# A planned attention and two-layer kernel: another bank for row transposes, regrouped sums, weight words moved, and the attention's norm shared and opened to ScalarE

## The chip, the core and the metric

One Trainium2 chip, one core. The metric is device microseconds of the whole program, median of the runs; the profiled execution is one more run, recorded by the hardware profiler, and it has a time of its own. Engines by their names in the profile: PE (TensorE's matmuls), PEld (its weight loads), DVE (VectorE), ACT (ScalarE), POOL (GpSimd), SP (SyncE, which issues nearly all DMAs here).

## What is computed

The reference, cut to what matters (`q`, `k`, `v` are 4 x 8 x 768 x 64; `x` is 3072 x 512; `w_in` 512 x 2048, `w_out` 2048 x 512, all float64 but the attention's inputs):

```python
for c in range(24):                      # chunks of 32 queries, with 8 memory keys
    k_full = concat(mem_k, k[max(0, 32*c - 16) : 32*c + 40])
    scores = (q_c @ k_full.T) / 8
    a = exp(scores - max(scores)); a = a / (sum(a) + 1e-9)
    out_c = a @ v_full
x = attention, as 3072 tokens x 512
h = x @ moe_w_in;  g = h * tanh(softplus(h));      x = g @ moe_w_out     # layer 1
h = x @ moe2_w_in; g = h * sigmoid(1.702 * h);     x = g @ moe2_w_out    # layer 2
```

The weights arrive as float64. The kernel takes their 32-bit words apart, rebuilds a float32 from them, and splits each float32 operand into a high and a low fp32r part; a product is then three matmuls (high x high, low x high, high x low).

## The kernel before

The program has four stages in time, on PE almost back to back.

- **Stage A** (to about 415 us): attention and layer 1's first product. `forward(j, f)` is one unit: 12 matmuls of 128x384 for token block j (8 blocks of 384) and column block f (16). It cycles over four PSUM banks, `h` twice, `o2`, `o3`. The attention of block j+1 runs between the units of block j, by *octs* (two heads x four windows of 96 queries) for j >= 2 and by *quads* (half an oct) for j < 2. An oct's steps are `oct_scores` (8 matmuls, L717), `quad` twice (mask and minimum on DVE, L758; four exponentials on ACT with their sums, L773; `plus` and `inverse`, L791 and L795, which turn the sums into factors; `norm`, L798, one DVE multiplication of 96x512, or `norm_act`, L807, four ACT instructions of 96x128), and `oct_out` (transposes L904, copies L911 or L913, values L924, and the split into `xh` and `xl`). For j >= 2 the norm could go to DVE alone.
- **Stage B** (about 415 to 685 us): layer 1's second product, `second(1, k)`, 12 units of 256 tokens. A unit is one 2x2 Winograd product: four blocks `a11`, `a12`, `a21`, `a22` are loaded from `g1d` and put through Mish on ACT, sums of them are formed by `comb` (L1226), each operand is split (L1235 or L1236, and L1238), and seven steps of 24 matmuls of 128x256 (L1248) run on PE. Step 1 writes bank `o3` (`hd`). At a unit's end `row` transposes its two result rows (tiles `ev` for the lower, `u` for the upper; four transposes each, L1268) into `o3` and `o2`; a copy to `u` (L1129 on ACT or L1130 on DVE) empties the bank and a DMA stores the row to `x1d`.
- **Stage C** (about 685 to 915 us): layer 2's first product, `first(q)`, 32 units of seven products (L1159).
- **Stage D** (to the end): layer 2's second product, `second(2, k)`, 12 units of the same seven steps, without Mish and without transposes.

`w_words(layer, part, p, ...)` makes one *set of words*: two loads of 512 KB of float64 weights, two conversions (a scaling on ACT, L346, or on DVE, L349; three integer operations on DVE, L355, L359, L363), four sums on DVE (L415), and in most sets four stores to `wd`. Twelve sets are placed in stage A (one every seven forward units from the 20th), six in stage B, six in stage C.

Order is set by `Plan`. Each operation has a rank, one or two ways (engine, cost), and tiles that it reads and writes; a tag such as `vt=2` says how many tiles rotate. `Plan.issue` plays the program through with those costs, picks on each engine the ready operation of the lowest rank, takes the second way only where the first engine's queue is long enough, and then emits everything in the order found. Each engine then works strictly in that order.

```python
bank = T[("o2", "o3")[th]].new([P, KD, P], F32)      # row(): th = 0 upper, 1 lower row
hd = T["o3"].new([P, H2], F32)                       # second(): step 1's bank
a11 = block(0, "vt", r - 2.6);  a22 = block(3, own[0], r - 1.9)
a21 = block(2, "vt", r - 1.2);  a12 = block(1, own[3], r - 0.6)
ways = [("dve", dve(4 * P), norm), ("act", 4 * act(P), norm_act)]
add(rank + 1.4, ways if j < EARLY else ways[:1], reads=[r, done], updates=[e])
```

Of the kernel before, what the change touches and what calls it, by code (L numbers as in the profile page):

```python
# [9 lines left out]
F32 = mybir.dt.float32  # L10
F32R = mybir.dt.float32r
I32 = mybir.dt.int32
AF = mybir.ActivationFunctionType
# [228 lines left out]
def kernel(  # L242
# [478 lines left out]
        add(rank + 0.5, [("pe", 1.4, scores)], reads=pair[0][2], writes=s)  # L721
        return s

    def quad(j, hp, gp, heads, rank, given=None):
        b, s0 = divmod(j * TB, S)
        g0 = s0 // GQ + 2 * gp
        queries, keys, turned_from = heads
# [6 lines left out]
        mx, sm = T["mx"].new([GQ, 2, 2], F32), T["sm"].new([GQ, 2, 2], F32)  # L734
        r = T["r"].new([GQ, 2, 2, 1], F32)
        done = fixed()

        def scores():
# [33 lines left out]
        def power(i, hh):  # L772
            nc.scalar.activation(  # L773
                out=e[:, i, hh, :],
                in_=e[:, i, hh, :],
                func=AF.Exp,
                scale=-1.0,
                bias=mx[:, i, hh:hh + 1],
                accum_out=sm[:, i, hh:hh + 1],
            )  # L780

        for i in range(2):
# [3 lines left out]
                    reads=[e, mx], writes=[done, sm], table="exp",  # L786
                )

        def plus():
            r3 = r.get().rearrange("p a b o -> p a (b o)")  # L790
            nc.vector.tensor_scalar(out=r3, in0=sm.get(), scalar1=1e-9, scalar2=None, op0=ALU.add)  # L791

        def inverse():
            r3 = r.get().rearrange("p a b o -> p a (b o)")
            nc.vector.reciprocal(out=r3, in_=r3)  # L795

        def norm():
            nc.vector.tensor_tensor(  # L798
                out=e.get(), in0=e.get(), in1=r.get().to_broadcast([GQ, 2, 2, P]), op=ALU.mult
            )  # L800

        add(rank + 1.4, [("dve", 0.23, plus)], reads=[sm], writes=[r])
        add(rank + 1.4, [("dve", 0.16, inverse)], updates=[r])
        def norm_act():
            for i in range(2):
                for hh in range(2):
                    nc.scalar.activation(  # L807
                        out=e[:, i, hh, :], in_=e[:, i, hh, :], func=AF.Copy, scale=r[:, i, hh, :]
                    )
# [136 lines left out]
    def quads():  # L946

        last = None
        for j in range(NB):
# [4 lines left out]
            for n in range(NQ):  # L954
                rank = base + 2 * n
                if j < EARLY:
                    gp, hp = divmod(n, H // 2)
                    if hp == 0:
                        st = rows_of_heads(j, gp, rank)
                    heads, vals = turned(j, hp, st, rank), st[2]  # L960
                else:
                    hp, gp = divmod(n, GB // 2)
                    if gp == 0:
                        pair = pair_of_heads(j, hp, rank)
                        if 2 * hp % HV == 0:
# [3 lines left out]
                        oct_out(j, hp, vals, rank, names, [  # L969
                            quad(j, hp, i, pair[i], rank + STAGGER * i, s)[1] for i in range(GB // 2)  # L970
                        ])
# [233 lines left out]
    def second(layer, k):  # L1205
# [93 lines left out]
        comb(r + 1.6, a22, a22, a11, ALU.subtract)  # L1299
        step(4, 1, a22, hb, False)  # L1300
        copy(r + 4.1, View(u2), hb, H2)
        step(5, 3, a11, hb, False)
        plus(r + 5.05, bottom, p5, hb)
        plus(r + 5.06, bottom, p4, hb, 0)
        row(1, bottom)
        comb(r + 2.4, a12, a12, a22, ALU.subtract)
        step(6, 6, a12, hc, False)
        plus(r + 6.1, top, u2, hc)
        row(0, top)
# [23 lines left out]
    for j in range(NB):  # L1333
        for f in range(NF):
# [4 lines left out]
            forward(j, f)  # L1339
            i = j * NF + f  # L1340
            n, rest = divmod(i - NF - 4, 7)
            if rest == 0 and 0 <= n < 12:
                layer, p = ((1, 4), (1, 5), (1, 6), (1, 7), (1, 0), (1, 1), (1, 2), (2, 0), (2, 1), (2, 2), (2, 3), (1, 3))[n]
# [8 lines left out]
            if i >= L1 - NF + 6 and f % 2 == 0:  # L1352
                w_out(1, f // 2 - 2, i + 1)
    w_out(1, 6, L1 + 0.5)
    for k1 in range(3 * NS):
        second(1, k1)
        if k1 % 2 == 0:
            p = (4, 5, 6, 7, 14, 15)[k1 // 2]
            w_words(2, p // NP, p % NP, RB[1] + 7 * k1 + 6, [pace[1, k1]], ("v", "v"))
# [54 lines left out]
```

## Time and profile before

| | |
|---|---|
| runs shown | 1161.67, 1163.86, 1165.37 us; median 1163.86 |
| profiled execution | 1165.48 us, its span 1163.7 us |
| PE busy | 1124.6 us (97%) |
| DVE busy | 867.2 us (75%) |
| ACT busy | 612.2 us (53%) |
| mean granted clock | 0.987 |
| chain that ended last | PE 87%, DMA 4%, DVE 3% |

PE's busy time and the chain both say that the program is PE's work from end to end; what is left to gain lies in PE's idle stretches and in the stretches in which its clock is at the lower of its two levels (1.2 instead of 2.4 GHz). The granted clock is given as a share of 2.4 GHz. A matmul's duration in the trace contains its way through the array, so two matmuls in a row overlap; what one costs is the distance from start to start.

### The profile page before, as it was taken

The numbers are of one execution on the slowest core, as the hardware profiler recorded it, in microseconds if no ns is written. First come the engines' busy times: TensorE is split into PE (matmuls) and PEld (weight loads), VectorE is DVE, ScalarE is ACT, GpSimd is POOL, SyncE is SP. The second block draws the span as 40 slices with busy tenths as digits, with TensorE's granted clock in tenths as the row PEclk, the third lists the DMA queues.
The fourth block names the chain that finished last, engine by engine and source line by source line (L and its number), as shares of the span: only waits on it lengthen the run. The fifth ranks groups of instructions, "written<-read, shape, count | busy, mean of one in ns | idle before, by whom it ended". The sixth has DMA issues, their size and how long they took to land.

```text
span 1163.7 us, 22807 instructions
## 1 busy us (share of the span) xinstructions
PE 1124.6 (97%) x8352; PEld 1091.0 (94%) x8352; DVE 867.2 (75%) x1975; ACT 612.2 (53%) x1416; POOL 15.1 (1%) x34
## 2 busy tenths in 40 slices
PE   7888999999999999999999899999999999999998
PEld 6677999999998999999999899999999999999998
DVE  5898878887876478788788876756466868787875
ACT  5775554565545446566565566556555534333332
POOL 2000000000000000000000000000000000000000
PEclk9899999999999999999999899999999999999999
DMA  9945778767894674754655577777878663635452
GB/s 210 263 128 141 198 213 245 206 158 206 239 245 123 184 210 127 207 165 128 204 168 154 177 232 243 236 255 228 261 243 267 208 172 101 163 109 157 116 138 62
DMA packets 325743, 217.97 MB, mean 187 GB/s; under 512 B 136120, under 2 KB 300743, under 8 KB 325631
## 3 DMA queue, kind: packets, MB, share of 16 engines
q1 hardware_dynamic: 325279, 215.76, 64.8%
q8 instruction: 66, 1.08, 0.4%
q0 software_dynamic: 352, 0.75, 0.3%
q14 instruction: 46, 0.38, 0.1%
HBM read 135.18 MB, written 81.26 MB: 186 GB/s over the span
## 4 chain that ended last, share of the span: by engine, by line
PE 87%; DMA 4%; DVE 3%; SPq 2%; ACT 2%; issue 1%; DVEq 0%; ACTq 0%
PE o L1248 18%; PE o L1004 12%; PE h L1004 11%; PE s L1248 11%; PE h L1248 11%; PE h L1159 8%; PE o L1159 7%; PE s L1159 3%; SPq L305 2%; PE o L717 1%; PE s L717 1%; PE o L924 1%; PE s L924 1%; PE s L904 1%; DMA vt<-in_v_dram 1%
## 5 line engine op out<-in xcount | busy, mean ns | idle before, releaser
L1004 PE MATMUL h<-xh,wi 128*128 128x384 f32 x384 | 102.3, 347 | 0.9 <-DVE gh L1130 0.8
L1004 PE MATMUL o<-xh,wi 128*128 128x384 f32 x384 | 101.6, 346 | 0.0
L773 ACT ACTIVATE e<-e,mx 96x128 f32<-96x128 f32 x240 | 93.1, 390 | 15.3 <-DVE mx L758 15.2
L1248 PE MATMUL o<-wo,xh 128*128 128x256 f32 x456 | 87.9, 288 | 6.8 <-ACT u L1129 4.2
L1238 DVE TENSOR_TENSOR xl<-wi,xh 128x1024 fp32r<-128x1024 f32 x64 | 77.8, 1220 | 6.7 <-ACT xh L1235 6.0
L1248 PEld LDWEIGHTS o<-wo,xh 128*128 128x128 f32 x456 | 72.3, 195 | 8.7 <-ACT u L1129 5.6
L1238 DVE TENSOR_TENSOR xl<-vt,xh 128x1024 fp32r<-128x1024 f32 x48 | 58.6, 1221 | 21.3 <-ACT xh L1235 20.6
L1004 PEld LDWEIGHTS h<-xh,wi 128*128 128x128 f32 x384 | 68.9, 191 | 3.6 <-ACT st L346 0.9
L1004 PEld LDWEIGHTS o<-xh,wi 128*128 128x128 f32 x384 | 69.7, 192 | 1.2
L1235 ACT ACTIVATE xh<-wi 128x1024 fp32r<-128x1024 f32 x51 | 53.9, 1058 | 29.2 <-PE h L1248 10.7
L1248 PE MATMUL o<-wo,xl 128*128 128x256 f32 x228 | 66.0, 290 | 1.2 <-DVE xl L1238 1.2
L1004 PE MATMUL o<-xl,wi 128*128 128x384 f32 x192 | 65.1, 339 | 0.0
L1004 PE MATMUL h<-xl,wi 128*128 128x384 f32 x192 | 65.1, 339 | 0.0
L1248 PE MATMUL s<-wo,xh 128*128 128x256 f32 x312 | 59.9, 287 | 1.2 <-DVE xh L1236 1.2
L1248 PE MATMUL o<-wi,xh 128*128 128x256 f32 x312 | 58.8, 282 | 0.0
L1248 PE MATMUL o<-wo,wi 128*128 128x256 f32 x342 | 48.4, 283 | 4.1 <-ACT u L1129 2.0
L1248 PEld LDWEIGHTS s<-wo,xh 128*128 128x128 f32 x312 | 49.4, 194 | 1.6 <-DVE xh L1236 1.6
L1248 PEld LDWEIGHTS o<-wo,wi 128*128 128x128 f32 x342 | 43.4, 188 | 6.2 <-ACT u L1129 2.7
L1129 ACT ACTIVATE e<-h 128x384 f32<-128x384 f32 (+1 forms) x50 | 22.4, 448 | 49.3 <-PE h L1248 37.9
L1248 PEld LDWEIGHTS o<-wi,xh 128*128 128x128 f32 x312 | 48.2, 190 | 0.0
L1248 PE MATMUL h<-wi,xh 128*128 128x256 f32 x256 | 47.6, 282 | 0.0
L1248 PE MATMUL h<-wo,xh 128*128 128x256 f32 x256 | 47.3, 281 | 0.0
(410 smaller groups left out, 3163.9 us busy)
## 6 DMA issues: line engine op xcount, KB each, us to landing
st<-in_moe_w_out_dram SPq DMA_DIRECT2D x32, 512.0 KB
st<-wd SPq DMA_DIRECT2D x29, 512.0 KB
g1d<-gh SPq DMA_DIRECT2D x64, 192.0 KB
g1d<-gl SPq DMA_DIRECT2D x64, 192.0 KB
vt<-g1d SPq DMA_DIRECT2D x24, 512.0 KB
wi<-g1d SPq DMA_DIRECT2D x24, 512.0 KB
vt<-gd SPq DMA_DIRECT2D x24, 512.0 KB
wi<-gd SPq DMA_DIRECT2D x24, 512.0 KB
```

Source lines behind the costliest of these rows:

```text
L305: queue.dma_start(out=o, in_=i)
L717: nc.tensor.matmul(out=s[hh][:, keys(d, i, True), :], lhsT=queries(d, i), rhs=keys(d, i), start=True, stop=True)
L773: nc.scalar.activation(out=e[:, i, hh, :], in_=e[:, i, hh, :], func=AF.Exp, scale=-1.0, bias=mx[:, i, hh:hh + 1], accum_out=sm[:, i, hh:hh ...
L904: nc.tensor.transpose(t[:, i, hh, :], e[:, i, hh, :], ident[:GQ, :GQ])
L924: nc.tensor.matmul(out=o[hh * D:(hh + 1) * D, g], lhsT=vt[:, g, h + hh], rhs=aTs[g // 2][:, g % 2, hh], start=True, stop=True,)
L1004: nc.tensor.matmul(out=h.get(), lhsT=a[:, c], rhs=b.at(kk), start=(n == 0), stop=(n == 3 * KD - 1))
L1129: ("act", act(n, True), lambda: nc.scalar.activation(out=dst(), in_=bank.get(), func=AF.Copy)),
L1159: nc.tensor.matmul(out=bank.get(), lhsT=a, rhs=b, start=(fresh and m == 0), stop=(m == 3 * K2 - 1), skip_group_check=not fresh,)
L1235: ("act", act(NP * P), lambda: nc.scalar.activation(out=flat(gh), in_=flat(src), func=AF.Copy)),
L1238: add(rank + 0.05, [("dve", dve(NP * P), lambda: nc.vector.tensor_tensor(out=flat(gl), in0=flat(src), in1=flat(gh), op=ALU.subtract))], re ...
L1248: nc.tensor.matmul(out=bank.get(), lhsT=a[:, p], rhs=b, start=(fresh and p == 0 and m == 0), stop=(p == NP - 1 and m == 2), skip_group_che ...
```

## The change

Four edits.

1. `row` of layer 1 transposes both rows into bank `o2`; `o3` is left to `hd` (and to the forward units of stage A).
2. Layer 1's sums are written into other tiles: `a22` becomes a21+a22, then that minus a11; `a21` becomes a11-a21; `a11` itself is only read. Layer 2's sums stay.
3. Stage A makes 14 sets of words instead of 12 (sets (2, 4) and (2, 5), of layer 2's first weights, at forward units 104 and 111); stage B makes four instead of six, behind units 1, 3, 5, 7 instead of 0, 2, 4, 6, 8, 10.
4. In an oct, `sm` and `r` are shared by its two quads: `inverses` runs once, on 96x8, behind the exponentials of both; the norms follow, each on DVE or on ACT, for every j.

```diff
+    def inverses(rank, sm, r):
...
+        add(rank + 1.4, [("dve", 0.23, plus)], reads=[sm], writes=[r])
+        add(rank + 1.4, [("dve", 0.16, inverse)], updates=[r])
...
-        ways = [("dve", dve(4 * P), norm), ("act", 4 * act(P), norm_act)]
-        add(rank + 1.4, ways if j < EARLY else ways[:1], reads=[r, done], updates=[e])
+        def scaled():
+            add(rank + 1.4, [("dve", dve(4 * P), norm), ("act", 4 * act(P), norm_act)], reads=[r, done], updates=[e])
+
+        if both:
+            return e, scaled
+        scaled()
...
+                        both = [T[x].new([GQ, GB, 2], F32) for x in ("sm", "r")]
+                        es = [quad(j, hp, i, pair[i], rank + STAGGER * i, s, both) for i in range(GB // 2)]
+                        inverses(rank + STAGGER, *both)
+                        for _, scaled in es:
+                            scaled()
...
-            bank = T[("o2", "o3")[th]].new([P, KD, P], F32)
+            bank = T["o2"].new([P, KD, P], F32)
...
-        comb(r + 0.2, a11, a11, a21, ALU.subtract)
-        comb(r + 0.3, a21, a21, a22, ALU.add)
-        step(3, 4, a21, hc, True)
+        if layer == 1:
+            comb(r + 0.3, a22, a21, a22, ALU.add)
+            comb(r + 0.4, a21, a11, a21, ALU.subtract)
+            s1, s2, s3 = a22, a11, a21
...
+        step(3, 4, s1, hc, True)
...
+        comb(r + (1.2, 1.6)[layer - 1], s2, a22, a11, ALU.subtract)
+        step(4, 1, s2, hb, False)
...
+        step(5, 3, s3, hb, False)
...
+        comb(r + 2.4, a12, a12, s2, ALU.subtract)
...
-            if rest == 0 and 0 <= n < 12:
+            if rest == 0 and 0 <= n < 14:
...
+    WB = {1: (0, 6), 3: (0, 7), 5: (1, 6), 7: (1, 7)}
...
-        if k1 % 2 == 0:
-            p = (4, 5, 6, 7, 14, 15)[k1 // 2]
+        if k1 in WB:
```

What moves, at three places. **PE between two units of stage B** (the fourth and the fifth): before, the last matmul of the fourth unit, its upper row's transposes (`u` into `o2`), step 0 of the next unit (`s0`), the lower row's transposes (`ev` into `o3`), and step 1 of the next unit (`o3`).

```order
L1248 MATMUL h_6380<-wi15_5613,xl_6491 128x256
L1268 MATMUL o2_6587<-ident_64,u_6483 128x128 x4
L1248 MATMUL s0_6596<-wo7_2846,wi1_6582 128x256 x2
...
L1248 MATMUL s0_6596<-wo3_4998,wi2_6585 128x256
L1268 MATMUL o3_6628<-ident_64,ev_6594 128x128 x4
L1248 MATMUL o3_6645<-wo6_2997,xh_6592 128x256 x2
```

Now, from the end of the next unit's step 0 on:

```order
L1259 MATMUL s0_6589<-wo3_5169,wi2_6587 128x256
L1279 MATMUL o2_6623<-ident_64,ev_6614 128x128 x4
L1259 MATMUL o3_6628<-wo6_3038,xh_6616 128x256 x2
...
L1259 MATMUL o3_6628<-wi7_5440,xl_6619 128x256
L1279 MATMUL o2_6667<-ident_64,u_6472 128x128 x4
L1259 MATMUL s0_6589<-wo4_2943,xh_6660 128x256 x2
```

Before, step 1 came directly behind transposes into its own bank; now a whole step stands between the two groups of transposes, which share `o2`, and step 1's bank is touched by no transposes. All eleven places between units read so now; before there were two kinds, this one and one in which `ev` and `u` follow each other directly, with step 1 behind them.

**DVE in an oct of stage A** (`r` and `sm` are the factors and sums, `e` the exponentials; `u`, `st` belong to a set of words). Before, two quads, each with its own small operations and its norm:

```order
L791 TENSOR_SCALAR r<-sm 96x4
L359 SCALAR_TENSOR_TENSOR u<-st,u 128x512
L795 RECIPROCAL r<-r 96x4
L363 SCALAR_TENSOR_TENSOR u<-st,u 128x512
L798 TENSOR_TENSOR e<-e,r 96x512
L791 TENSOR_SCALAR r<-sm 96x4
L795 RECIPROCAL r<-r 96x4
L798 TENSOR_TENSOR e<-e,r 96x512
```

Now, an oct on DVE, and then ACT's rows around the other half of its norm (`gl` and `gh` are forward units' results):

```order
L727 TENSOR_SCALAR r<-sm 96x8
L359 SCALAR_TENSOR_TENSOR v<-st,v 128x512
L730 RECIPROCAL r<-r 96x8
L363 SCALAR_TENSOR_TENSOR v<-st,v 128x512
L804 TENSOR_TENSOR e<-e,r 96x512
```

```order
L784 ACTIVATE e,sm<-e,mx 96x128 x4
L1140 ACTIVATE gl<-h 128x384
L812 ACTIVATE e<-e,r 96x128 x4
L1140 ACTIVATE gh<-o_3659 128x384
```

One pair of small operations is left of two, and one of the two norms stands on ACT, behind the second quad's exponentials. Over the program 20 of the 48 quads of octs have their norm on ACT now (none before); the other 28 stay on DVE.

**PE at the end of the attention** (the last oct's scores L717, transposes L904, values L924; L1004 are forward units). Before:

```order
L717 MATMUL o_5169<-kT,qT 96x128
L1004 MATMUL o_5179<-xh,wi_1302 128x384 x2
...
L1004 MATMUL o_5206<-xl,wi_1374 128x384
L1248 MATMUL s_5240<-wo_2846,xh 128x256 x2
...
L1248 MATMUL s_5240<-wo_4998,xl 128x256
L904 MATMUL o_5270<-ident,e 128x96 x4
L904 MATMUL o_5275<-ident,e 128x96 x4
L924 MATMUL o_5284<-aT,vt 64x96 x8
L1004 MATMUL h<-xh,wi_576 128x384 x2
```

Now:

```order
L717 MATMUL o_5015<-kT,qT 96x128
L932 MATMUL s_5032<-aT,vt 64x96 x8
L1015 MATMUL h<-xh,wi_999 128x384 x2
...
L1015 MATMUL h<-xl,wi_1194 128x384
L912 MATMUL o_5162<-ident,e 128x96 x4
L912 MATMUL o_5171<-ident,e 128x96 x4
L1015 MATMUL h<-xh,wi_1233 128x384 x2
...
L932 MATMUL o_5199<-aT,vt 64x96 x8
L1015 MATMUL o_5215<-xh,wi_1302 128x384 x2
```

Before, two forward units and the first step of stage B (`s`, L1248) stood between the last scores and their transposes; now it is five forward units, a sixth lies between transposes and values, two more behind the values, and the step of stage B has gone behind the last forward unit.

## Rows read from the trace of the kernel before

**Rows 1.** Busy time by stretch: PE, PEld, DVE, ACT, POOL, clock, DMA share, GB/s.

```profile
100.00:200.00 100.00, 99.63 (x780) 93.97 (x780) 78.57 (x320) 52.16 (x200) 2.10 (x7) 0.99 0.76 207
450.00:650.00 200.00, 192.71 (x1604) 190.03 (x1603) 160.93 (x200) 119.77 (x154) 0.00 (x0) 1.00 0.57 166
940.00:1140.00 200.00, 199.89 (x1682) 199.63 (x1682) 154.80 (x160) 72.19 (x103) 0.00 (x0) 1.00 0.48 133
```

**Rows 2.** Waits of PE, 430 to 690 us (total, times, longest); PE in order of time.

```profile
PE o L1248 <- ACT u L1129: 6.2, 9, 1.2
PE o L1248 <- DVE u L1130: 1.3, 1, 1.3
...
478.62 0.60 PE L1268 MATMUL o<-ident,ev 128*128 128x128 f32 x4
479.05 0.60 PE L1268 MATMUL o<-ident,u 128*128 128x128 f32 x4
479.90 1.68 PE L1248 MATMUL o<-wo,wi 128*128 128x256 f32 x12 [0.25 <-ACT u L1129]
...
500.57 0.60 PE L1268 MATMUL o<-ident,ev 128*128 128x128 f32 x4
502.25 0.51 PE L1248 MATMUL o<-wo,xh 128*128 128x256 f32 x2 [1.09 <-ACT u L1129]
```

**Rows 3.** PE between the eleventh and twelfth unit of stage B, and the stretches there.

```profile
652.52 0.66 PE L1268 MATMUL o<-ident,ev 128*128 128x128 f32 x4 [0.41 <-DVE ev L1277]
654.60 0.54 PE L1248 MATMUL o<-wo,xh 128*128 128x256 f32 x2 [1.42 <-DVE xh L1236]
656.33 0.58 PE L1248 MATMUL o<-wo,xl 128*128 128x256 f32 x1 [1.19 <-DVE xl L1238]
...
655.00:660.00 5.00, 3.81 (x18) 3.67 (x18) 5.00 (x8) 0.70 (x1) 0.00 (x0) 0.50 0.38 118
660.00:665.00 5.00, 5.00 (x37) 5.00 (x37) 3.57 (x4) 2.25 (x5) 0.00 (x0) 0.82 0.46 134
```

**Rows 4.** PE at the end of the attention, and the stretch there.

```profile
372.87 0.51 PE L1248 MATMUL s<-wo,xh 128*128 128x256 f32 x2 [1.25 <-DVE xh L1236]
374.13 0.39 PE L1248 MATMUL s<-wo,xl 128*128 128x256 f32 x1 [0.75 <-DVE xl L1238]
379.82 0.88 PE L924 MATMUL o<-aT,vt 128*64 128x96 f32 x16 [0.63 <-ACT aT L911]
...
375.00:380.00 5.00, 4.37 (x29) 4.18 (x30) 0.86 (x2) 0.87 (x2) 0.00 (x0) 0.66 0.00 0
```

**Rows 5.** Groups of instructions on DVE, 100 to 375 us: busy, mean ns | idle.

```profile
L798 DVE TENSOR_TENSOR e<-e,r 96x512 f32<-96x512 f32 x46 | 31.0, 673 | 0.5
L359 DVE SCALAR_TENSOR_TENSOR u<-st,u 128x512 int32<-128x512 int32 x12 | 8.2, 683 | 0.1
L791 DVE TENSOR_SCALAR r<-sm 96x4 f32<-96x4 f32 x47 | 7.1, 151 | 0.0
L355 DVE TENSOR_SCALAR u<-u 128x512 int32<-128x512 int32 x12 | 5.0, 417 | 0.0
L415 DVE TENSOR_TENSOR v<-v 128x256 f32<-128x256 f32 x12 | 4.8, 401 | 0.0
```

**Rows 6.** Line 807, the norm on ACT: ns min/median/max, first and last start.

```profile
L807 ACT ACTIVATE e<-e,r x28: 385/390/404, 14.9 to 87.0; 96x128 f32<-96x128 f32 x28
```

**Rows 7.** PE before 100 us: transposes that wait for the factors.

```profile
97.82 0.52 PE L827 MATMUL o<-ident,e 96*128 96x96 f32 x4 [1.88 <-DVE r L791]
```

**Rows 8.** One oct amid stage A in order of time: its scores, its last norm.

```profile
221.83 1.12 PE L717 MATMUL o<-kT,qT 64*96 64x128 f32 x16
...
229.30 0.65 DVE L798 TENSOR_TENSOR e<-e,r 96x512 f32<-96x512 f32 x1
```

**Rows 9.** The chain that ended last: two forward units, one step.

```profile
385.06 4.16 PE o L1004 x24
...
1091.18 2.86 PE h L1248 x24
```

More of the change, by code (lines that the diff above doesn't have):

```diff
@@ L722, in oct_scores, with plus, inverse, quad @@
         return s
-    def quad(j, hp, gp, heads, rank, given=None):
+    def inverses(rank, sm, r):
+        def plus():
+            nc.vector.tensor_scalar(out=r.get(), in0=sm.get(), scalar1=1e-9, scalar2=None, op0=ALU.add)
+        def inverse():
+            nc.vector.reciprocal(out=r.get(), in_=r.get())
+        add(rank + 1.4, [("dve", 0.23, plus)], reads=[sm], writes=[r])
+        add(rank + 1.4, [("dve", 0.16, inverse)], updates=[r])
+    def quad(j, hp, gp, heads, rank, given=None, both=None):
         b, s0 = divmod(j * TB, S)
@@ L733, in quad @@
         e = T["ev" if j == 0 and hp % 2 else "e"].new([GQ, 2, 2, P], F32)
-        mx, sm = T["mx"].new([GQ, 2, 2], F32), T["sm"].new([GQ, 2, 2], F32)
-        r = T["r"].new([GQ, 2, 2, 1], F32)
+        mx = T["mx"].new([GQ, 2, 2], F32)
+        sm, r = both or [T[n].new([GQ, 2, 2], F32) for n in ("sm", "r")]
         done = fixed()
@@ L778, in power @@
                 bias=mx[:, i, hh:hh + 1],
-                accum_out=sm[:, i, hh:hh + 1],
+                accum_out=sm[:, first + i, hh:hh + 1],
             )
@@ L787, in quad @@
                 )
[L789 to L795, printed above, removed]
+        if not both:
+            inverses(rank, sm, r)
         def norm():
             nc.vector.tensor_tensor(
-                out=e.get(), in0=e.get(), in1=r.get().to_broadcast([GQ, 2, 2, P]), op=ALU.mult
-            )
-        add(rank + 1.4, [("dve", 0.23, plus)], reads=[sm], writes=[r])
-        add(rank + 1.4, [("dve", 0.16, inverse)], updates=[r])
+                out=e.get(), in0=e.get(), op=ALU.mult,
+                in1=r[:, first:first + 2].unsqueeze(3).to_broadcast([GQ, 2, 2, P]),
+            )
         def norm_act():
@@ L807, in norm_act @@
                     nc.scalar.activation(
-                        out=e[:, i, hh, :], in_=e[:, i, hh, :], func=AF.Copy, scale=r[:, i, hh, :]
+                        out=e[:, i, hh, :], in_=e[:, i, hh, :], func=AF.Copy, scale=r[:, first + i, hh:hh + 1]
                     )
-        ways = [("dve", dve(4 * P), norm), ("act", 4 * act(P), norm_act)]
-        add(rank + 1.4, ways if j < EARLY else ways[:1], reads=[r, done], updates=[e])
+        def scaled():
[3 more added lines that the diff above has]
+        scaled()
         return after, e
@@ L968, in quads @@
                         s = oct_scores(pair, rank, names)
-                        oct_out(j, hp, vals, rank, names, [
-                            quad(j, hp, i, pair[i], rank + STAGGER * i, s)[1] for i in range(GB // 2)
-                        ])
+                        both = [T[x].new([GQ, GB, 2], F32) for x in ("sm", "r")]
[3 more added lines that the diff above has]
+                            scaled()
+                        oct_out(j, hp, vals, rank, names, [e for e, _ in es])
                     yield
@@ L1294, in second @@
         copy(r + 2.1, View(top, slice(0, H2)), ha, H2)
-        comb(r + 0.2, a11, a11, a21, ALU.subtract)
-        comb(r + 0.3, a21, a21, a22, ALU.add)
-        step(3, 4, a21, hc, True)
+        if layer == 1:
+            comb(r + 0.3, a22, a21, a22, ALU.add)
+            comb(r + 0.4, a21, a11, a21, ALU.subtract)
+            s1, s2, s3 = a22, a11, a21
+        else:
+            comb(r + 0.2, a11, a11, a21, ALU.subtract)
+            comb(r + 0.3, a21, a21, a22, ALU.add)
+            s1, s2, s3 = a21, a22, a11
+        step(3, 4, s1, hc, True)
         copy(r + 3.1, View(p5), hc, H2)
-        comb(r + 1.6, a22, a22, a11, ALU.subtract)
-        step(4, 1, a22, hb, False)
+        comb(r + (1.2, 1.6)[layer - 1], s2, a22, a11, ALU.subtract)
+        step(4, 1, s2, hb, False)
         copy(r + 4.1, View(u2), hb, H2)
-        step(5, 3, a11, hb, False)
+        step(5, 3, s3, hb, False)
         plus(r + 5.05, bottom, p5, hb)
@@ L1341 @@
             n, rest = divmod(i - NF - 4, 7)
[L1342 to L1343 removed]
+            if rest == 0 and 0 <= n < 14:
+                layer, p = ((1, 4), (1, 5), (1, 6), (1, 7), (1, 0), (1, 1), (1, 2), (2, 0), (2, 1), (2, 2), (2, 3), (1, 3), (2, 4), (2, 5))[n]
                 tiles = None
@@ L1354 @@
     w_out(1, 6, L1 + 0.5)
+    WB = {1: (0, 6), 3: (0, 7), 5: (1, 6), 7: (1, 7)}
     for k1 in range(3 * NS):
         second(1, k1)
-        if k1 % 2 == 0:
-            p = (4, 5, 6, 7, 14, 15)[k1 // 2]
-            w_words(2, p // NP, p % NP, RB[1] + 7 * k1 + 6, [pace[1, k1]], ("v", "v"))
+        if k1 in WB:
+            part, p = WB[k1]
+            w_words(2, part, p, RB[1] + 7 * k1 + 6, [pace[1, k1]], ("v", "v"))
         if k1 in (9, 10):
```

1 line of the change is left out of this document (removed).

## The prediction

> **What bounds the kernel now.** I read the busy times by stretch first, then who PE waits for, then PE in order of time. In stage A's body PE is busy 99.6 of 100 us, in stage D 199.9 of 200, and in stage B 192.7 of 200 [rows 1]: PE bounds the program, and time can only come from where it idles or runs at its lower clock. Those places are three: the ends of stage B's units, the last of those ends, and the end of the attention. Stage C's order of work is the same on PE in both kernels but for its first products, and stage D's is wholly the same, so I give both no gain. The profiled execution took 1165.48 us, 1.62 above the median of the runs shown; the sum is made against it and the 1.62 taken off at the end. A measurement of this kernel can tell about 0.3%, 3.5 us, from no change.
>
> **The change part by part.**
>
> *The bank.* In stage B PE waits ten times for a copy that empties a bank of row transposes, 6.2 us for ACT and 1.3 for DVE [rows 2]. The rows in order show why: four transposes of `ev` go to `o3`, and the next work on PE, step 1 of the following unit, writes `o3` too; it starts 1.68 us after the transposes (500.57 to 502.25), where the transposes of `u`, which need another bank, start only 0.43 behind those of `ev`. That place loses 1.25 us, of which the trace books 1.09 as idle; the rest is the overlap of two matmuls that a wait destroys, 0.16 to 0.17 each time (the other kind, 479.05 to 479.90, loses 0.42 with 0.25 booked). So the term is 7.5 + 10 x 0.16 = **9.1 us**. With both rows in `o2`, step 1 waits for no copy. What is late next is the copy out of `o2` before `u` is transposed. One step, 2.86 us [rows 9], lies in between, and the copy was over within 1.68 even in the slow kind; so I price the new wait near nothing. Its bounds are 0 and the old price, 1.25 at each place.
>
> *Fewer words in stage B.* Between the eleventh and the twelfth unit PE waits 0.41 + 1.42 + 1.19 = 3.0 us, every time for DVE: for the row's sum, then for both parts of a split [rows 3]. Three lost overlaps add 0.5. The clock falls to its lower level behind this: 0.50 over 655 to 660 and 0.82 over the next 5, which loses 2.5 + 0.9, less 0.6 for the part of the last wait that lies in it: 2.8. Together **6.3 us**. DVE is busy without a pause there. A set of words costs DVE 2 x (0.42 + 0.68 + 0.68) + 4 x 0.40 = 5.2 us [rows 5], where the third integer operation is taken as the second. Before, one set fell due just behind the eleventh unit; now the last falls due behind the eighth. I expect the whole 6.3; the bounds are 0 (the preparation of stage C's operands stays there) and 6.3.
>
> The two sets that move to stage A bring it 10.4 us of DVE work, four loads of 512 KB and eight stores, all issued by SP. They fall due at forward units 104 and 111, near the end of the attention, where DVE is busy 0.9 of 5 us and the DMA engines move nothing [rows 4]; that covers them. If the cover is gone, the weights of stage C come late, not those of stage B. Price 0, at worst 5.2.
>
> *The sums.* The seven steps and four sums are the same in number; `a11`'s tile is free about two steps earlier, so its next load starts earlier. No wait of PE in stage B names a load, so I price it at 0; the bounds are 0 and a gain of 1.
>
> *The attention.* Sharing removes 24 of each kind of small operation, about 0.15 each, and 20 norms leave DVE, 20 x 0.67 = 13.5 us [rows 5]. ACT takes 80 instructions of 0.39, 31 us [rows 6], beside 52% busy time [rows 1]. None of that is on PE's path, where stage A's body idles for 0.4%. What counts is whether the transposes still find their operand. The first quad's norm now waits for the second quad's exponentials. In the oct of [rows 8] the scores end at 222.95 and the second quad's norm at 229.95, 7.0 us later. The changed order puts four forward units of 2.08 us [rows 9] or more between an oct's last scores and its transposes (for the first oct three, and other work): 8.3 us and up. So 1.3 us stay, and the price is 0; the upper bound is below, under the rivals.
>
> First the row: a norm costs 0.67 on DVE and 4 x 0.39 = 1.56 on ACT. The Trainium skill (ScalarE: Activation LUTs, Rules for kernel authors) says to multiply on VectorE, not on ScalarE. The row agrees on the price. By that rule the 20 norms lose 20 x (1.56 - 0.67) = 17.8 us and the sum would be 1163; by the row of the stretch ACT has that time to spare, and I stay with the sum as made.
>
> *The end of the attention.* Before, PE reaches stage B's first step early and waits there 1.25 + 0.75, then 0.63 for the last oct's copy; three overlaps add 0.5; the clock is 0.66 over 375 to 380, 1.7 us less 0.3 for the last wait in it [rows 4]. That is **4.5 us**. In the changed order five forward units stand there (10.4 us, against the 7.0 that an oct takes), a sixth covers the copies, and the step is gone to the end of the stage. I expect all of it; the bounds are 0 and 4.5.
>
> *The sum.* 9.1 + 6.3 + 4.5 = 19.9 us. For new small waits I put 1.5 against it: stage D, with DVE at 77% and the same steps, waits for almost nothing (0.1 in 200 us [rows 1]), and half of ten small waits of 0.42 would be 2.1. Stage B's DVE stays near its 80%: shorter units raise it by a twentieth, two sets fewer lower it by as much. So 1165.5 - 19.9 + 1.5 = 1147.1 for the profiled execution, and **1145.5** for the median.
>
> **The rivals.**
>
> *Only the bank pays.* The waits at the twelfth unit and at the end of the attention come from DVE being late at a crowded spot, and a plan that packs PE closer may meet the next such spot. For it: DVE is as full in stage B as before. Against it: both spots lose their cause by name. 1163.9 - 9.1 = 1154.8.
>
> *The shared bank is the new wait.* The copy of `ev`'s bank stands in ACT's order behind Mish operations and splits; if it is more than 2.86 us late, PE waits at `u`'s transposes. Ten times the old 1.25 gives 1145.5 + 12.5 = 1158. Against it: in the slow kind the copy ended 1.68 us behind the transposes.
>
> *ACT becomes the late engine, and nothing is left of the gain.* Twenty times 0.89 us of longer norms reach PE through copies that queue behind them: 1145.5 + 17.8 = 1163.3, no change. Against it: ACT is half idle in stage A, and forward units have four banks to wait in. This is where the Trainium skill's rule would lead.
>
> *Slower: the attention waits at every oct.* One factor operation for both quads makes each oct's transposes wait for its last exponential. Before 100 us one such wait, for the factors, took 1.88 us [rows 7]. At 24 octs, with the lost overlap, that is 24 x 2.04 = 49 us, 1145.5 + 49 = 1194. It decides from 1 us an oct (19.9 + 3.5 over 24). Against it: the 8.3 us and more that the order leaves.
>
> **How the numbers follow.** Forecast 0.64; only the bank 0.18; shared bank 0.08; ACT late 0.05; slower 0.05. The range runs from 1140, if the waits around 97 us [rows 7] and the 1.5 go too, to 1157, which takes in the second case and most of the way to the third. Faster 0.88 (the first three, less some spill), same 0.06, slower 0.06.
>
> **What would show it.** Right: no wait of PE on a copy to `u` between units of stage B, its units 20.9 us apart from step 1 to step 1 (7 x 2.86 and two groups of transposes at 0.43), where 479.90 to 502.25 is 22.35; the clock at 1.00 around the twelfth unit and at the end of the attention; stage C starting some 19 us earlier; the 24 octs without waits at their transposes. Wrong: waits of PE on ACT at the transposes of `u`, splits on DVE named as releasers in more than one or two places of stage B, or PE idle in stage A's body above 1 us in 100.

## The result, and the profile after

The change runs in 1146.17 us (median of four runs, 1144.98 to 1147.05) against 1164.61 for the kernel before on the same chip: ratio 0.9844 [0.9823, 0.9866], 18.2 us faster. The forecast was 1145.5. The total and the three places hold; how the gain divides over the edits does not, and that is what the experiments are about.

The profiled execution took 1144.98 us (span 1143.2, 20.5 less than before). Stretches of the changed kernel, in the columns of [rows 1]:

```profile
100.00:200.00 100.00, 100.00 (x774) 92.90 (x775) 74.58 (x309) 58.34 (x226) 2.95 (x7) 0.98 0.77 207
430.00:630.00 200.00, 198.77 (x1677) 198.32 (x1676) 163.83 (x195) 131.01 (x174) 0.00 (x0) 1.00 0.56 171
...
920.00:1120.00 200.00, 199.92 (x1680) 199.42 (x1679) 153.61 (x160) 72.27 (x103) 0.00 (x0) 1.00 0.48 132
640.00:645.00 5.00, 5.00 (x45) 5.00 (x44) 4.75 (x6) 3.75 (x7) 0.00 (x0) 1.00 0.17 52
645.00:650.00 5.00, 5.00 (x42) 5.00 (x41) 5.00 (x6) 3.56 (x6) 0.00 (x0) 1.00 0.18 56
...
365.00:370.00 5.00, 5.00 (x38) 4.71 (x39) 2.96 (x7) 2.22 (x5) 0.00 (x0) 1.00 1.03 367
```

In stage B PE's busy time went from 192.7 to 198.8 of 200 us, and at the two places that [rows 3] and [rows 4] show with a granted clock of 0.50, 0.82 and 0.66 (they now come 10 to 16 us earlier: the twelfth unit's start and the end of the attention) it is 1.00 (2.4 GHz). Stage D is as it was. All waits of PE from 405 to 690 us (total, times, longest):

```profile
PE h L1259 <- DVE xl L1249: 0.9, 1, 0.9
PE o L1170 <- DVE wo L471: 0.5, 1, 0.5
PE s L1259 <- DVE xl L1249: 0.3, 1, 0.3
```

No copy to `u` is among them; [rows 2] have 7.5 us of these. The three that are there make 1.7 us, 0.5 of it in stage C, where the prediction put 1.5 of new small waits. PE in order of time, two units of stage B and the start of the twelfth:

```profile
493.57 0.60 PE L1279 MATMUL o<-ident,ev 128*128 128x128 f32 x4
496.86 0.60 PE L1279 MATMUL o<-ident,u 128*128 128x128 f32 x4
...
514.39 0.60 PE L1279 MATMUL o<-ident,ev 128*128 128x128 f32 x4
517.69 0.60 PE L1279 MATMUL o<-ident,u 128*128 128x128 f32 x4
...
638.38 0.39 PE L1259 MATMUL o<-wo,xh 128*128 128x256 f32 x2
...
641.23 0.60 PE L1279 MATMUL o<-ident,ev 128*128 128x128 f32 x4
641.58 0.36 PE L1259 MATMUL o<-wo,xh 128*128 128x256 f32 x1
```

From row to row these units are 20.82 us apart (20.9 was named as the sign). At the twelfth unit the order has changed as well. Before, that place was of a third kind: both groups of transposes came first, and the matmul at 654.60 in [rows 3], which waits, begins step 0 (its eight groups all take their weights from `wo`; in step 1 four take `wo` and four `wi`). Step 1 followed at 661.19:

```profile
661.19 0.63 PE L1248 MATMUL o<-wo,xh 128*128 128x256 f32 x2
```

Now step 0 stands ahead of the transposes (638.38), step 1 starts 0.35 us behind them (641.58), and neither waits. At the end of the attention, PE in order of time:

```profile
354.51 1.12 PE L717 MATMUL o<-kT,qT 64*96 64x128 f32 x16
...
366.91 0.82 PE L912 MATMUL o<-ident,e 96*128 96x96 f32 x8
369.77 0.88 PE L932 MATMUL o<-aT,vt 128*64 128x96 f32 x16
```

The last oct's transposes come 12.4 us after its scores and wait for nothing. The place of [rows 7] kept its price under another name:

```profile
98.71 0.52 PE L835 MATMUL o<-ident,e 96*128 96x96 f32 x4 [1.89 <-ACT wi L383]
```

**Where the 20.5 us came from.** Four anchors divide the span: the first scores of an oct behind the first forward units, the first step 1 of stage B, the first step 1 of stage D, and the end. They are these rows, of the kernel before and of the changed one:

```profile
92.04 1.21 PE L717 MATMUL s<-kT,qT 64*96 64x128 f32 x10
...
414.83 0.39 PE L1248 MATMUL o<-wo,wi 128*128 128x256 f32 x1 [0.58 <-ACT gl L1129]
...
920.62 0.51 PE L1248 MATMUL o<-wo,wi 128*128 128x256 f32 x2 [0.43 <-ACT wi L1235]
```

```profile
92.93 0.89 PE L717 MATMUL s<-kT,qT 64*96 64x128 f32 x4
...
411.08 0.52 PE L1259 MATMUL o<-wo,wi 128*128 128x256 f32 x3
...
899.93 0.51 PE L1259 MATMUL o<-wo,wi 128*128 128x256 f32 x2 [0.43 <-ACT wi L1246]
```

Their differences, for the kernels that ran (us of one profiled execution each; the last three are under "Pairs and halves"):

| kernel | to the first scores | stage A from there | stages B and C | stage D |
|---|---|---|---|---|
| before | 92.0 | 322.8 | 505.8 | 243.1 |
| changed | 92.9 | 318.2 | 488.9 | 243.3 |
| bank only | 91.8 | 322.2 | 500.4 | 242.6 |
| words only | 92.9 | 325.2 | 499.9 | 242.8 |
| attention only | 93.1 | 318.2 | 505.0 | 243.5 |
| sums only | 92.7 | 321.0 | 497.0 | 242.7 |
| bank and sums | 94.4 | 322.8 | 492.9 | 242.8 |
| all but the bank | 94.4 | 318.0 | 498.4 | 243.3 |
| all but the words | 92.6 | 318.6 | 492.9 | 243.5 |
| all but the sums | 92.7 | 319.4 | 494.0 | 244.3 |
| all but the attention | 92.9 | 325.4 | 491.9 | 244.4 |
| one sum's place undone | 90.8 | 317.3 | 493.0 | 244.1 |
| octs' norms on DVE | 93.0 | 319.1 | 490.6 | 243.2 |
| octs' norms on ACT | 92.5 | 318.0 | 489.9 | 243.4 |

Stage A gave 4.6 us, B and C 16.9, the start lost 0.9. Within B and C, eleven units (to step 1 of the twelfth, 661.19 and 641.58) took 15.9 us less, 0.35 of it for a group of transposes that now stands behind that step, and the rest 1.1 less. Single executions of one kernel differ by 2 to 6 us in all, so the table shows the stage in which an edit acts; its size is read from the ratios.

### The profile page after: what moved, and what is told of

Read it like the earlier page. It is cut to its first block, busy times and chain, and to the rows that moved or that the text cites. A ratio compares the mean times of both kernels' runs of the same rounds, so it can differ in the third digit from the quotient of the medians.

```text
span 1143.2 us, 22801 instructions
## 1 busy us (share of the span) xinstructions
PE 1116.8 (98%) x8352; PEld 1085.2 (95%) x8352; DVE 849.1 (74%) x1909; ACT 636.9 (56%) x1495; POOL 16.9 (1%) x33
## 4 chain that ended last, share of the span: by engine, by line
PE 90%; DVE 3%; SPq 2%; DMA 2%; ACT 1%; issue 1%; DVEq 0%; ACTq 0%
PE o L1259 17%; PE o L1015 12%; PE h L1015 12%; PE h L1259 11%; PE s L1259 11%; PE h L1170 9%; PE o L1170 8%; PE s L1170 4%; SPq L305 2%; PE o L717 1%; PE s L717 1%; PE o L932 1%; PE s L932 1%; DMA vt<-in_v_dram 1%; PE o L1279 1%
## 5 line engine op out<-in xcount | busy, mean ns | idle before, releaser
L1249 DVE TENSOR_TENSOR xl<-vt,xh 128x1024 fp32r<-128x1024 f32 x48 | 58.3, 1221 | 18.9 <-ACT xh L1246 18.2
L1246 ACT ACTIVATE xh<-wi 128x1024 fp32r<-128x1024 f32 x50 | 52.6, 1054 | 20.5 <-PE h L1259 9.1
L784 ACT ACTIVATION_READ_ACCUMULATOR e<-e,mx 96x1 f32 x240 | 46.0, 192 | 0.0
```

Of the source, the lines that this page charges most:

```text
L784: nc.scalar.activation(out=e[:, i, hh, :], in_=e[:, i, hh, :], func=AF.Exp, scale=-1.0, bias=mx[:, i, hh:hh + 1], accum_out=sm[:, first + ...
L1246: ("act", act(NP * P), lambda: nc.scalar.activation(out=flat(gh), in_=flat(src), func=AF.Copy)),
L1249: add(rank + 0.05, [("dve", dve(NP * P), lambda: nc.vector.tensor_tensor(out=flat(gl), in0=flat(src), in1=flat(gh), op=ALU.subtract))], re ...
```

## The experiments

Each kernel is compared with the kernel before on its own chip; a difference of 0.001 in the ratio is 1.2 us. The theory to test is the prediction's division: bank 9.1, words 6.3, sums 0, attention's end 4.5. The rival is that the edits remove one another's waits. Every edit makes `Plan` lay out the order anew, so what an edit is worth here is its worth with the order that comes with it. Where a worth is the difference of two ratios, its uncertainty is some 3 us.

### One edit undone in the changed kernel

The bank:

```diff
-            bank = T["o2"].new([P, KD, P], F32)
+            bank = T[("o2", "o3")[th]].new([P, KD, P], F32)
```

> The changed kernel with the first edit undone: the lower row's transposes go to bank o3 again. The plan now puts the transposes of ev and u directly behind each other at all eleven places between units, with the next unit's step 1, which writes o3, right behind them. Theory (step 1 waits for the copy that empties o3): each place costs what the same kind cost in the kernel before, 0.42 us (0.25 booked as a wait on ACT), so 11 x 0.42 = 4.6 us on the changed kernel's 1146.2, about 1151, and up to 1155 if some places show the longer wait of 1.25. Rival (the waits came from a full VectorE, the bank is only where they were booked): no wait of PE on a copy to u, and 1146 to 1147.

Measured: 1154.65 us, 0.9885 [0.9865, 0.9904], so the bank is worth 0.0041, 4.8 us, when it comes last. Waits of PE from 405 to 690 us:

```profile
PE o L1259 <- ACT u L1140: 1.7, 5, 0.7
PE s L1259 <- DVE xl L1249: 1.5, 2, 1.1
PE o L1259 <- DVE u L1141: 0.9, 1, 0.9
```

The waits on copies return, but as 2.6 us in six places, not the 7.5 in ten of [rows 2]: another edit holds the rest down. Nine of the eleven places are of the cheap kind of [rows 2] (`ev` and `u` back to back); the other two, of the dear kind, have the longest of these waits, 0.9 and 0.7.

The words:

```diff
-            if rest == 0 and 0 <= n < 14:
+            if rest == 0 and 0 <= n < 12:
...
-        if k1 in WB:
-            part, p = WB[k1]
-            w_words(2, part, p, RB[1] + 7 * k1 + 6, [pace[1, k1]], ("v", "v"))
+        if k1 % 2 == 0:
+            p = (4, 5, 6, 7, 14, 15)[k1 // 2]
+            w_words(2, p // NP, p % NP, RB[1] + 7 * k1 + 6, [pace[1, k1]], ("v", "v"))
```

> The changed kernel with the third edit undone: twelve sets of words in stage A, six in stage B behind units 0, 2, 4, 6, 8, 10. Theory (the set behind the eleventh unit made VectorE late at the twelfth): PE waits for VectorE again between the eleventh and the twelfth unit, the clock falls to its lower level there, and up to 6.3 us come back, 1150 to 1152.5. Rival (with the bank free, PE no longer meets VectorE late): no such wait, 1146 to 1147.5.

Measured: 1148.81 us, 0.9844 [0.9829, 0.9858], the ratio of the whole change. Between the eleventh and the twelfth unit nothing waits although the words are back (one split in the twelfth's step 2 makes PE wait 0.7). As the last edit the words are worth 0.0 us, with some 3 us of uncertainty; the 4 us that the table's row has in B and C may be the spread between executions.

The sums:

```diff
-        if layer == 1:
-            comb(r + 0.3, a22, a21, a22, ALU.add)
-            comb(r + 0.4, a21, a11, a21, ALU.subtract)
-            s1, s2, s3 = a22, a11, a21
+        comb(r + 0.2, a11, a11, a21, ALU.subtract)
+        comb(r + 0.3, a21, a21, a22, ALU.add)
...
-        comb(r + (1.2, 1.6)[layer - 1], s2, a22, a11, ALU.subtract)
+        comb(r + 1.6, a22, a22, a11, ALU.subtract)
```

> The changed kernel with the second edit undone: layer 1's sums in their old tiles. Theory (no wait of PE in stage B names a load, so the earlier release of a11's tile is worth nothing): 1146 to 1147.2. Rival (the earlier release starts the next unit's loads in time and is part of the gain): PE waits for Mish or splits that wait for loads in stage B, 0.3 us or more at each of eleven places, 1149.5 and above.

Measured: 1152.3 us, 0.9873 [0.9858, 0.9888]: the sums are worth 3.4 us with some 3 us of uncertainty, where 0 was priced. PE waits from 405 to 690 us:

```profile
PE o L1279 <- ACT u L1140: 1.4, 2, 0.7
PE s L1259 <- DVE wi L1249: 1.2, 2, 1.0
PE o L1259 <- DVE xl L1249: 0.9, 2, 0.8
PE o L1279 <- DVE ev L1288: 0.9, 1, 0.9
```

The wait of 0.9 for `ev` is for the row itself: there its transposes stand directly behind the step that ends its sum. The two waits on `u` are for the shared bank. In both places the plan puts the two groups of transposes next to each other; the second waits until ACT has copied the first out of `o2`:

```profile
432.04 0.60 PE L1279 MATMUL o<-ident,ev 128*128 128x128 f32 x4
433.33 0.66 PE L1279 MATMUL o<-ident,u 128*128 128x128 f32 x4 [0.69 <-ACT u L1140]
```

```profile
432.68 0.60 ACT L1140 ACTIVATE u<-o 128x512 f32<-128x512 f32 x1
```

So the prediction's rival of the shared bank does show here, at two places of eleven. The other waits, 2.4 us, are of steps for splits. The expected sign of late loads, a wait at each of eleven places, is not there.

The attention (of a longer edit, the piece that decides where the factors are made and the norms may run):

```diff
-                        both = [T[x].new([GQ, GB, 2], F32) for x in ("sm", "r")]
-                        es = [quad(j, hp, i, pair[i], rank + STAGGER * i, s, both) for i in range(GB // 2)]
-                        inverses(rank + STAGGER, *both)
...
-            add(rank + 1.4, [("dve", dve(4 * P), norm), ("act", 4 * act(P), norm_act)], reads=[r, done], updates=[e])
+        ways = [("dve", dve(4 * P), norm), ("act", 4 * act(P), norm_act)]
+        add(rank + 1.4, ways if j < EARLY else ways[:1], reads=[r, done], updates=[e])
```

> The changed kernel with the fourth edit undone: factors by quad, norms of blocks from the third on by VectorE alone. The plan now leaves two forward units between the last oct's scores and its transposes instead of five. Theory (the end of the attention was worth 4.5 us, and the fourth edit's order is what cures it): PE waits there again, with a fall of the clock, 1148.5 to 1151; stage A's body stays without waits. Rival (that gain came from the moved first step of stage B, which this plan also places behind the attention): 1146 to 1147.

Measured: 1155.41 us, 0.9899 [0.9885, 0.9913]: 6.4 us, and 7.2 in stage A of the table's row, where 4.5 was named. PE and DVE in order of time, then the stretches:

```profile
373.99 0.52 PE L904 MATMUL o<-ident,e 96*128 96x96 f32 x4 [1.49 <-DVE e L798]
376.00 0.76 PE L904 MATMUL o<-ident,e 96*128 96x96 f32 x4 [1.49 <-DVE e L798]
378.38 1.55 PE L924 MATMUL o<-aT,vt 128*64 128x96 f32 x16 [1.63 <-ACT aT L911]
```

```profile
374.85 0.39 DVE L355 TENSOR_SCALAR v<-v 128x512 int32<-128x512 int32 x1
375.16 0.68 DVE L798 TENSOR_TENSOR e<-e,r 96x512 f32<-96x512 f32 x1
375.77 0.68 DVE L359 SCALAR_TENSOR_TENSOR v<-st,v 128x512 int32<-128x512 int32 x1
```

```profile
370.00:375.00 5.00, 3.02 (x19) 2.54 (x17) 5.00 (x16) 3.58 (x15) 0.00 (x0) 1.00 0.30 72
375.00:380.00 5.00, 2.38 (x21) 1.89 (x21) 4.21 (x7) 1.07 (x3) 0.00 (x0) 0.61 0.60 218
380.00:385.00 5.00, 5.00 (x29) 5.00 (x30) 1.15 (x2) 0.57 (x2) 0.00 (x0) 0.70 0.65 181
```

The norms that PE waits for stand in DVE's order among the integer operations of the two sets of words that moved to stage A (lines 355 and 359). The stretch that the prediction named as their cover, with DVE busy 0.86 of 5 us [rows 4], has it busy 4.21 here, and in the 5 us before it DVE is busy throughout (3.38 in the kernel before); the waits are 4.6 us where they were 2.6. The clock falls behind them, to 0.61 and 0.70. Stage A takes 325.4 us against the 322.8 of before: with the attention's old end, the moved words cost 2.6 us.

### One edit alone, in the kernel before

The same edits the other way round. The bank alone:

> The kernel before with the first edit alone. Its plan has the order ev, step 1, u at all places between units; the end of the attention is as before. Theory (the bank's wait is worth 9.1 us by itself): ratio 0.9915 to 0.993 to the kernel before, no wait of PE on a copy to u, the waits at the end of the attention unchanged. Rival (the four edits pay only together): ratio 0.996 to 1.0, waits on VectorE in place of those on the copies.

Measured: 1160.79 us, 0.9965 [0.9952, 0.9979]: 4.1 us, not 9.1. The waits of step 1 on copies are gone; the largest in their place, from 405 to 690 us:

```profile
PE o L1268 <- DVE ev L1277: 4.1, 4, 1.3
PE o L1248 <- DVE xl L1238: 2.0, 3, 1.0
PE s L1248 <- DVE wi L1238: 1.6, 2, 1.4
```

The order is not the expected one at all places. At four of the eleven, the four waits for `ev`, the plan puts the row's transposes ahead of step 0 and directly behind the step that ends the row's sum on DVE:

```profile
497.20 0.63 PE L1268 MATMUL o<-ident,ev 128*128 128x128 f32 x4 [0.94 <-DVE ev L1277]
```

Before, `u` and step 0, or step 0 alone, stood between the two and gave DVE the time; only at the twelfth unit it was `u` alone, and there PE waited 0.41 for `ev` too [rows 3]. One place has the wait for the shared bank (0.8, for DVE's copy to `u`, where `u` follows `ev` directly). The clock at the twelfth unit stays at 1.00 in this run.

The words alone:

> The kernel before with the third edit alone. My first theory (the set behind the eleventh unit causes the 6.3 us there) gives a ratio of 0.994 to 0.996. The theory after the run that put the sets back without a loss (the sets are worth nothing; the wait at the twelfth unit came from how the plan fell there) gives 0.998 to 1.002, the copies' waits unchanged.

Measured: 1162.71 us, 0.9983 [0.9973, 0.9994]: 2.0 us. The twelfth unit's waits for the split are gone as predicted and its clock is 1.00, but the waits on copies stand at 9.1 us instead of 7.5 (1.4 of them at the twelfth unit's step 1), and stage A loses 2.4 at the same place as above (3.0 us for DVE's `e`, 1.4 for ACT's `aT`).

The attention alone:

> The kernel before with the fourth edit alone. Its plan has five forward units between the last oct's scores and its transposes. Theory (the fourth edit cures the end of the attention, 4.5 us in the kernel before, and nothing else): ratio 0.995 to 0.997, no wait of PE and no fall of the clock there, stage B as before. Rival (the sharing slows stage A's body or moves the wait): 0.998 or above.

Measured: 1163.53 us, 0.9985 [0.9975, 0.9995]: 1.7 us. In the table stage A gives the predicted 4.6. PE has no wait from 365 to 420 us, but further on the waits on copies are 7.8 us in ten places, the twelfth unit's stand, and splits make new ones of 1.2. B and C take 505.0 us against 505.8, so nothing of the gain is given back there in this execution. The profiled run, 1161.47, is one of the shortest of twelve; the ratio's 1.7, with some 1.2 of uncertainty, is less than the table's 4.6, and the record does not show where the rest goes.

The sums alone:

> The kernel before with the second edit alone. Theory after the run that put the sums back and lost some 3.5 us (the earlier release of a11's tile lets Mish, and the splits behind it, come in time): ratio 0.996 to 0.998, with the copies' waits still there in the kind that costs 0.42 us each, which this plan has at ten of eleven places. Rival (the sums matter only when the bank's wait is gone, since that wait covers them): the gain is that of the kind of place alone, 5 x 0.83 = 4.2 us, and shows as shorter waits on the copies, with VectorE's and ScalarE's lateness as before.

Measured: 1157.67 us, 0.9932 [0.9917, 0.9946]: 7.9 us (7.3 by the medians), the largest of the four, from the edit that I had priced at 0, and more than either theory gave. PE's first wait by size from 405 to 690 us, then a place of it in order of time:

```profile
PE o L1248 <- ACT u L1129: 2.9, 7, 1.0
```

```profile
477.04 0.60 PE L1268 MATMUL o<-ident,ev 128*128 128x128 f32 x4
477.47 0.60 PE L1268 MATMUL o<-ident,u 128*128 128x128 f32 x4
478.32 0.38 PE L1248 MATMUL o<-wo,wi 128*128 128x256 f32 x1 [0.25 <-ACT u L1129]
```

With both banks kept, ten of eleven units now end in the cheap kind of place of [rows 2], `ev` and `u` back to back, mostly with 0.25 booked or nothing, and no longer in the dear kind with 1.09. The twelfth unit's waits for DVE are gone too. SyncE's queue and ACT show what was late there. Before:

```profile
644.78 1.02 SPq L305 DMA_DIRECT2D wd<-v  x1
645.87 0.65 SPq L305 DMA_DIRECT2D vt<-g1d  x1
```

```profile
652.23 1.06 ACT L1218 ACTIVATE vt<-vt 128x1024 f32<-128x1024 f32 x1 [0.95 <-DMA vt<-g1d]
```

The two loads of `vt` for the twelfth unit, that of `a11` among them, are issued from 8.7 us ahead of step 0 (654.60) on, which uses `a11` and waits. Mish on ACT waits for the load until 652.23, and the split that PE waits for comes behind Mish. With the sums alone the two are issued from 635.95 on, 10.8 us ahead of step 0 at 646.78, which does not wait; with the words alone it is 10.4 us, again without a wait of step 0. The sums alone:

```profile
635.95 2.78 SPq L305 DMA_DIRECT2D vt<-g1d  x2
```

So the split that PE waited for was late because its load was, though the wait names DVE. What held the load back is open: ahead of it stand a store of the words in the queue (644.78) and DVE's split of an old `vt` tile (644.52 for 1.23 us), which ends 0.1 us before the first issue.

One correction to "The change": `a11` is not only read. The code sets `s1, s2, s3 = a22, a11, a21`, so the second sum goes into the tile of `a11`, and that tile is free one step earlier than before, not about two.

### Pairs and halves

The bank and the sums, without the words and the attention:

> The kernel before with the edits of the bank and of the sums only; attention and words as before. Alone the two gave -4.2 and -7.3 us. Theory 'both take away the same waits': the copies' waits are gone, each edit being worth less beside the other, so 7 to 10 us of gain, ratio 0.991 to 0.994. Theory 'together more than the sum': the bank alone turned the copies' waits into late sums and splits on DVE, and the new sums give DVE the slack; then more than 11.5 us, ratio below 0.990, and between 430 and 640 us PE waits under 2 us in all. The waits at the end of the attention, some 4.5 us, stay in both.

Measured: 1152.77 us, 0.9894 [0.9875, 0.9913]: 12.3 us, where the two alone make 12.0. So the two neither double nor overlap by more than the measurement shows. All waits from 405 to 690 us are 4.4 us (1.9 between 430 and 640), none for a copy to `u`, and none for a row (`ev`) either. PE's order fits: with both edits all eleven places read step 0, `ev`, step 1, `u`, in this kernel and in every other one that has the two but that with the words put back (nine). With the sums undone three of the eleven differ, with the bank alone five. With the attention added (all but the words, 0.9844) it is 18.2. These three edits make the whole gain, within some 3 us.

Which part of the sums' edit acts: the new tiles, with the second sum left at its old place:

```diff
-        comb(r + (1.2, 1.6)[layer - 1], s2, a22, a11, ALU.subtract)
+        comb(r + 1.6, s2, a22, a11, ALU.subtract)
```

> The changed kernel with the new sums, but the second of them (s2, which the product with a11 begins with) left at its old place in the order of the work, 1.6 instead of 1.2. Undoing all of the edit of the sums cost 3.4 us. If the tiles are what matters (a22 and a11 take the sums, a21 is free otherwise), the ratio stays at the changed kernel's 0.984 to 0.985; if the earlier place of that sum is what matters, it goes back most of the way to 0.987, and PE waits again for copies at transposes and for splits between 430 and 640 us.

Measured: 1150.37 us, 0.9874 [0.9854, 0.9893], as with the whole edit undone (0.9873). This speaks for the earlier place of that sum. It is not settled: the intervals of this run and of the change touch, its five runs lie between 1146.86 and 1151.69, and the profiled one is the shortest. In that execution B and C take 493.0 us, near the 494.0 with the whole edit undone, but its eleven places have the order of the change, its waits from 405 to 690 us are 2.9 us against 1.7, and all but the words, with the change's ratio, took 492.9.

Which part of the attention's edit acts: the factors shared, the norms of the octs on DVE alone (20 of them go back to it):

```diff
-            add(rank + 1.4, [("dve", dve(4 * P), norm), ("act", 4 * act(P), norm_act)], reads=[r, done], updates=[e])
+            add(rank + 1.4, [("dve", dve(4 * P), norm), ("act", 4 * act(P), norm_act)][:1 if both else 2], reads=[r, done], updates=[e])
```

> The changed kernel with the norms of the octs on DVE alone; the factors stay shared by two quads. It separates the two halves of the attention's edit, which was worth 6.4 us when it was undone last. Theory 'ACT's help pays': DVE was late at the end of the attention because of the norms, so 13.5 us of DVE work come back in stage A, the waits at the end of the attention come back, and the ratio to the kernel before is near 0.990, as with the whole edit undone (0.9899). Theory 'sharing pays': the fewer small operations and the order with the factors in one place are what moves the transposes back; then no wait comes back and the ratio stays near 0.985. The order has four forward units ahead of the last oct's transposes, one fewer than the changed kernel.

Measured: 1148.64 us, 0.9862 [0.9844, 0.988]: 2.1 us of the 6.4 go, within the measurement's uncertainty, and stage A takes 319.1 us against 325.4 with the whole edit undone. PE waits 1.3 us for ACT's `aT` and never for a norm. So the larger part of the worth lies in the shared factors and the order that comes with them; these two are not separated.

All norms of the octs on ACT:

```diff
-            add(rank + 1.4, [("dve", dve(4 * P), norm), ("act", 4 * act(P), norm_act)], reads=[r, done], updates=[e])
+            add(rank + 1.4, [("act", 4 * act(P), norm_act)] if both else [("dve", dve(4 * P), norm), ("act", 4 * act(P), norm_act)], reads=[r, done], updates=[e])
```

> The changed kernel with every oct's norm on ACT (four operations of 0.39 us each), none on DVE. By the rival of the prediction 'ACT becomes the late engine' (and by the page's rule to multiply on VectorE) each norm moved costs 1.56 - 0.67 = 0.89 us; with some 28 more of them moved, that would be 25 us more than the changed kernel, about 1171 us and a ratio near 1.006, and PE would wait for ACT in stage A. By my theory ACT has that time to spare where 58% of it is busy, and forward units stand between: 0 to 2 us more, ratio 0.984 to 0.987, and no new waits of PE between 100 and 365 us.

Measured: 1146.23 us, 0.9842 [0.9823, 0.9861], the same as the change. A stretch, and PE's only wait from 100 to 365 us:

```profile
100.00:200.00 100.00, 100.00 (x777) 92.79 (x776) 71.74 (x302) 69.28 (x265) 1.57 (x6) 0.99 0.76 197
```

```profile
PE o L861 <- ACT aT L841: 0.6, 1, 0.6
```

ACT is busy 69 of 100 us and PE still 100. The planner moved other work to DVE in exchange: by the counts of instructions (ACT 90 more, DVE 6 fewer) 28 norms went to ACT and some 22 operations the other way. The Trainium skill (ScalarE: Activation LUTs, Rules for kernel authors) would have the multiply on VectorE; here four operations of 0.39 us in place of one of 0.67 cost nothing, since neither engine bounds the stretch.

## Why the prediction was right, and where its steps were wrong

**The places and the sum.** PE is the bound, and the places that paid are the ones that were named. In stage B, up to step 1 of the twelfth unit, it was 15.5 us without the transposes that moved; the bank's 9.1 and the twelfth unit's 6.3, less 1.5, make 13.9; the other 1.6 is not traced. The end of the attention gave 4.6 in stage A, where 4.5 was named. From that step 1 to stage D, to which I gave no gain, it was 1.1: in stage C two waits for DVE, 0.66 and 0.71, are gone and one of 0.49 is new. The start lost 0.9 with the same instructions in the same order, so this is spread between executions. As far as the places go, the total is no luck. In the division over the edits it is: the bank and the words were put too high, the sums too low, and these errors cancel.

**The bank, 9.1.** Its waits were rightly named, and in the whole change they are gone. But the term holds only in the order of the whole change. Alone the edit gives 4.1 us, since at four places the plan puts `ev` directly behind the step that ends its sum, and PE waits 4.1 us for the row; as the last edit it gives 4.8, since the sums' edit turns most places into the cheap kind. "What is late next" was asked of the copy out of `o2`, with a step in between. The row itself was late, and where the plan left no step in between, the copy too: 0.7 to 0.8 us each, at two places with the sums undone and at one with the bank alone.

**Fewer words in stage B, 6.3.** The waits for the split at the twelfth unit do go with the words, but they go with the sums too, and the fall of the clock there, 2.8 of the 6.3, is absent with the bank alone, the words alone and the sums alone. So the term can't be given to the words: alone 2.0, last 0.0. The price of the two sets moved to stage A, put at 0 with 5.2 at worst, is 2.4 to 2.6 us where the attention's old end stands, and about 0 where it is changed.

**The sums, 0.** This step failed: 7.9 us alone, 3.4 last. Its premise, that no wait of PE names a load, was read too literally; the split at the twelfth unit was late by its load. And with these sums the plan ends units in another kind of place (ten of eleven cheap ones alone, and with the bank nearly always the order of the change), which I hadn't priced. Whether the new tiles or the earlier place of one sum does it is open.

**The attention, 0, and its end, 4.5.** Right in place and in stage A's size. With the other edits it is worth 6.4, since it also takes away the collision with the moved words; alone 1.7, less than stage A shows, which stays open.

**The rivals.** "Only the bank pays" is out; so is the shared bank's copy as a new wait in the change itself (it shows where an edit is missing), ACT as the late engine (even with 28 norms more), and waits at every oct (one of 0.6 us from 100 to 365).

## What to carry to other kernels

Where PE is full and two engines run just behind it, read the waits for the place and its worth, and credit a place to the change, not to the one edit that seems to cure it: the words, priced at a third of the gain, added nothing measurable at the end. Before a wait is priced as gained, look where the new order puts the work that waited: here the row's transposes waited wherever they stood directly behind the step that ends their sum. Before moved work is priced at nothing, ask whether it falls due in the idle stretch or ahead of it, among the work that PE waits for. A wait that names a split may be a late load: go two steps back.

## What was not expected of the hardware

All fourteen kernels have the same instructions in the same order on every engine up to their first scores, and reach these at 90.8 to 94.4 us: a spread of 3.6 us at the start, larger than some of the edits, so differences of single executions are read from an anchor behind it. With the attention undone, PE idled 4.6 us in three waits between 372 and 378 us, none longer than 1.63, and the granted clock was 0.61 and then 0.70 in the two stretches of 5 us that hold the end of these waits and the work behind them: 5 x 0.39 + 5 x 0.30 = 3.45 us of clock on top of the waits, at most, as some of it falls into a wait. At the twelfth unit of the kernel before, behind three waits of 3.0 us in all, it was 0.50 [rows 3]; with the bank alone, where three waits there make 2.3 us (1.25, 0.82 and 0.24), it stayed at 1.00.
